# Down projection in a retention-plus-MLP kernel: a seven-product scheme exchanged for another with chained sums

## The chip, the cores and the metric

The kernel runs on one NeuronCore of one Trainium2 chip. TensorE (PE, with its weight loads listed apart as PEld) multiplies, VectorE (DVE) and ScalarE (ACT) do elementwise work and empty PSUM, GpSimd (POOL) issues the loads, and SyncE (SP) issues stores and DMA transposes. The metric is the device time in microseconds, the median of several executions. Before the change it is 288.92 us (288.50 to 289.43 over three executions).

## The reference

```python
# retention: batch 8, heads 8, seq 576, head dim 64
scores = q @ k.T / 8 * Dmat          # Dmat[i, j] = gamma_h ** (i - j) for i >= j, else 0
x = (scores @ v) -> [4608, 512]      # tokens x (heads * dim)
# MLP: d_model 512, d_ff 2048
h = x @ w_in                         # [4608, 2048]
g = h * sigmoid(1.702 * h)
out = g @ w_out                      # [4608, 512], float32
```

The change concerns only the last line, the down projection.

## The kernel before

The 4608 tokens are 36 units of 128, and four units make a chunk of 512 tokens, so there are nine chunks. The retention of later units is worked out ahead, in pieces placed between the products of the MLP (`block`, `ahead`). For a chunk the up projection (`up`, L560) takes 16 blocks f of 128 rows of d_ff: four matmuls for each f into PSUM bank A or B in turn, and then ACT's GELU (L569) from that bank into `gT[:, f, tokens]`. With two banks, block f+2 can only start when the GELU of block f has read its bank.

The down projection of chunk 0 is plain (`down`, L588). From chunk 1 on it works by seven products instead of eight. The g of a chunk is a 2x2 block matrix G: the row is the half of the tokens (`raw(row, ...)`), the column the parity of f. W (w_out) is a 2x2 block matrix too: the row is the parity of f, the column the half of the 512 outputs (`wpart`). A `product` (L673) is 16 matmuls of 128x256 for a pair of two units a half, eight matmuls for a pair of one unit a half; with `more` it is added onto what the bank holds. With `late=1` the matmuls that need the last f come at its end. `turn()` deals the banks A and B alternately. Chunks 1 to 7 are one `Pair` of two units in each half. Chunk 8 is two pairs with one unit in each half, and the last pair stores half rows (`halves=True`), those of row 1 through ACT's queue.

`run` (L701) is the order of the seven products. In the version before, the sums of w_out (`wsums`, five for each quarter of w_out, worked out during chunk 0) and of g (`sums`, five for each call: three into `gsum`, two in place in `gT`) are all independent of one another. In `run`, ACT copies three products or sums of products out of PSUM into `osb` (`copy`, L696), and DVE does six additions and subtractions (`comb`, L699), through a scratch tile `wtmp`. The last instruction on a pair's results is the `comb` of quarter (0, 0), on DVE.

Between the products stand the calls `hook(0)` to `hook(6)`. They issue pieces of the retention work: `x_out_pair` (L552), `scores_out` (L514) and `state_sum` (L449) on DVE, `state_cast` (L458) on ACT, and matmuls on PE. In chunks 2 to 7, `hook(0)` casts what was summed before, `hook(2)` issues a block on PE, hooks 2 to 5 two of its DVE pieces each, and `hook(6)`, behind the last product, calls `cast_now()`: a cast on ACT of the states of the next two units. That is one unit after chunk 2 (128x512) and two units after chunks 3 to 6 (128x1024); after chunks 1 and 7 hook 6 has no cast.

The order on each engine is the order in which the program calls `op`; there is no planner. `Program.op` (L41) derives the waits from the names that an operation reads and writes: every wait is a semaphore wait in front of the instruction. A value read from an earlier instruction of the same engine is waited for as well (except on PE); a mere overwrite on the same engine is not. An engine does not go past an instruction that waits. SP and ACT wait in the same way for the instruction that fills a row before they issue its store.

Of the kernel before, what the change touches and what calls it, by code (L numbers as in the profile page):

```python
# [17 lines left out]
NF = FF // P  # L18
# [11 lines left out]
class Program:  # L30
# [10 lines left out]
    def op(self, eng, fn, reads=(), writes=(), dma=None, ndma=1, after_ops=()):  # L41
        o = Op()
        o.eng, o.fn, o.dma, o.signal, o.count = eng, fn, dma, False, None
        o.idx = len(self.streams[eng]) + 1
        deps = {}
        for k in reads:
            for d in self.writers.get(k, ()):
                deps[id(d)] = (d, True)
        for k in writes:
            for d in self.writers.get(k, ()) + self.readers.get(k, ()):  # L50
                deps.setdefault(id(d), (d, False))
        known = self.known[eng]
        need = []
        for d, raw in deps.values():
            if d.dma is None:
                if d.eng == eng and dma is None and (eng == "pe" or not raw):
                    continue
                agent, val = d.eng, d.idx
            else:
                agent, val = d.dma, d.dval  # L60
            need.append((agent, val, d))
        for d in after_ops:
            need.append((d.eng, d.idx, d))
        need.sort(key=lambda x: -x[1])
        waits = {}
        for agent, val, d in need:
            if known.get(agent, 0) >= val:
                continue
            if agent in waits and waits[agent][0] >= val:
                continue  # L70
            waits[agent] = (val, d)
        pruned = []
        for agent, (val, d) in waits.items():
            if any(
                a2 != agent and d2.known.get(agent, 0) >= val
                for a2, (_, d2) in waits.items()
            ):
                continue
            pruned.append(d)
        for agent, (val, d) in waits.items():  # L80
            d.signal = True
            known[agent] = max(known.get(agent, 0), val)
            for a2, v2 in d.known.items():
                if v2 > known.get(a2, 0):
                    known[a2] = v2
        o.waits = pruned
        o.known = dict(known)
        if dma is None:
            o.known[eng] = max(o.known.get(eng, 0), o.idx)
        else:  # L90
            self.dma_count[dma] = self.dma_count.get(dma, 0) + 16 * ndma
            o.dval = self.dma_count[dma]
            o.known[dma] = o.dval
        self.streams[eng].append(o)
        for k in writes:
            self.writers[k] = (o,)
            self.readers[k] = ()
        for k in reads:
            self.readers[k] = self.readers.get(k, ()) + (o,)
        return o  # L100
# [60 lines left out]
def bass_retnet_parallel__then__act_gelu_quick_kernel(  # L161
# [10 lines left out]
    with es:  # L172
        def sb(name, shape, dtype):
            return es.enter_context(nc.sbuf_tensor(name, shape, dtype))
# [14 lines left out]
        xT = [sb(f"xT{i}", [P, 4, 512], BF16) for i in range(2)]  # L189
        gT = sb("gT", [P, NF, 512], BF16)  # L190
        gsum = sb("gsum", [P, 3, NF // 2, 256], BF16)
        wsum = sb("wsum", [P, 5, NF // 2, 256], BF16)
        wtmp = sb("wtmp", [P, 512], FP32)
        warmt = sb("warmt", [P, 512], BF16)
        tblt = sb("tblt", [P, 4], BF16)
        gq = sb("gq", [P, 6, 4, P], FP32)
# [16 lines left out]
        op = pr.op  # L213
# [381 lines left out]
        def store(u, n0=0, n1=DM, eng="sp"):  # L595
            i = u % 4

            def f(e):
                return [
                    e.dma_start(out[S * bb + s0 : S * bb + s0 + n, n0:n1], osb[p0 : p0 + n, i, n0:n1])  # L600
                    for p0, n, bb, s0 in unit_rows(u)
                ]
            o = op(eng, f, reads=okeys(i, n0, n1), writes=[f"out{u}_{n0}"],
                   dma=f"d_o{i}_{n0}", ndma=len(unit_rows(u)))
            last_store[o.dma] = o
# [13 lines left out]
        def wpart(r, c):  # L619
            return lambda k: (w_out_sb[:, 2 * k + r, 256 * c : 256 * c + 256], f"wout{k // 2}")  # L620

        def wsums(i):
            def part(r, c):
                return w_out_sb[:, 4 * i + r : 4 * i + 4 : 2, 256 * c : 256 * c + 256]

            for n, (x, y, alu) in enumerate((
                ((0, 0), (1, 1), ALU.add), ((0, 0), (0, 1), ALU.add), ((1, 0), (1, 1), ALU.add),
                ((0, 1), (1, 1), ALU.subtract), ((1, 0), (0, 0), ALU.subtract),
            )):
                op("dve", lambda e, n=n, x=x, y=y, alu=alu: e.tensor_tensor(  # L630
                    wsum[:, n, 2 * i : 2 * i + 2, :], part(*x), part(*y), alu),
                   reads=[f"wout{i}"], writes=[f"ws{n}_{i}"])

        def wsummed(n):
            return lambda k: (wsum[:, n, k, :], f"ws{n}_{k // 2}")

        class Pair:
# [14 lines left out]
                        for j in range(self.r[row], self.r[row] + self.nt)]  # L652

            def sums(self, f0, f1):
                a, g = (lambda r, c: self.gpart(r, c, f0, f1)), (lambda r, c: self.gkeys(r, c, f0, f1))
                for n, x, y in ((1, (1, 0), (1, 1)), (2, (0, 0), (0, 1)), (0, (0, 0), (1, 1))):
                    op("dve", lambda e, n=n, x=x, y=y: e.tensor_tensor(  # L657
                        gsum[:, n, f0 // 2 : f1 // 2, self.at : self.at + self.n], a(*x), a(*y), ALU.add),
                       reads=g(*x) + g(*y), writes=[f"gs{n}_{k}_{j}" for j in self.places() for k in range(f0 // 2, f1 // 2)])
                for x, y in (((1, 0), (0, 0)), ((0, 1), (1, 1))):  # L660
                    op("dve", lambda e, x=x, y=y: e.tensor_tensor(a(*x), a(*x), a(*y), ALU.subtract),  # L661
                       reads=g(*x) + g(*y), writes=g(*x))

            def raw(self, row, col):
                def f(k, t):
# [22 lines left out]
            def bank(self, b):  # L688
                return bank[b][:, 0 : 256 * self.nt].rearrange("p (t n) -> p t n", t=self.nt), [b]

            def tmp(self):
                w = wtmp[:, 2 * self.at : 2 * self.at + 256 * self.nt]
                return w.rearrange("p (t n) -> p t n", t=self.nt), [f"wtmp{j}" for j in self.places()]

            def copy(self, dst, src):
                op("act", lambda e: e.activation(dst[0], src[0], AF.Copy), reads=src[1], writes=dst[1])  # L696

# [3 lines left out]
            def run(self, c, hook, halves=False):  # L701

                a, b = turn(), turn()
                q, A, B, W = self.quarter, self.bank(a), self.bank(b), self.tmp()
                add, sub = ALU.add, ALU.subtract

                def give(row, col, whole):
                    for j in range(self.r[row], self.r[row] + self.nt):
                        if halves:
                            store(4 * c + j, 256 * col, 256 * col + 256, "act" if row else "sp")  # L710
                        elif whole:
                            store(4 * c + j)

                self.product(a, self.raw(1, 1), wsummed(4), late=1)
                self.copy(q(1, 1), A)
                hook(0)
                self.product(b, self.raw(0, 0), wsummed(3))
                self.comb(W, B, q(1, 1), add)
                hook(1)
                self.product(a, self.summed(1), wpart(0, 0), True)  # L720
                self.copy(q(1, 0), A)
                give(1, 0, False)
                hook(2)
                self.comb(q(1, 1), W, q(1, 0), sub)
                self.product(b, self.summed(2), wpart(1, 1), True)
                self.copy(q(0, 1), B)
                give(0, 1, False)
                hook(3)
                self.comb(q(0, 0), W, q(0, 1), sub)
                self.product(a, self.summed(0), wsummed(0))  # L730
                self.comb(q(1, 1), A, q(1, 1), add)
                hook(4)
                self.product(b, self.raw(1, 0), wsummed(1))
                self.comb(q(1, 1), B, q(1, 1), add)
                give(1, 1, True)
                hook(5)
                self.product(a, self.raw(0, 1), wsummed(2), True)
                self.comb(q(0, 0), A, q(0, 0), add)
                give(0, 0, True)
                hook(6)  # L740
                turn()

# [3 lines left out]
        def turn():  # L746
            turns[0] += 1
            return "BA"[turns[0] % 2]
# [351 lines left out]
```

## Time and profile before

| | |
|---|---|
| median of three executions | 288.92 us |
| the profiled execution, its own time | 290.05 us |
| its span, first to last instruction | 288.2 us |
| PE busy | 277.5 us, 96% |
| DVE busy | 187.8 us, 65% |
| ACT busy | 130.3 us, 45% |
| mean granted TensorE clock | 0.994 |
| sums of g (L657, L661) on DVE | 32.1 + 21.9 us |
| combinations (L699) on DVE, 54 of them | 34.0 us |
| copies (L696) on ACT, 27 of them | 14.8 us |

The 34.0 us are the five groups of L699 in the groups by line: 11.3 + 8.9 + 8.2 + 3.1 + 2.5. In such a listing a row has the line, the engine, what is written and read, the count, the time that the engine was busy with it, and the idle time ahead of it with what ended it. In a timeline a row has the start, the length, the engine, the line and the operation, and in brackets how long the engine had been idle and for whom. In the chain of waits a row has the start and the time that the step adds to the chain. The modelled end of a matmul lies past the start of the next one, so spacing on PE is read from starts.

### The profile page before, as it was taken

What the parts mean: (1) busy time and instruction counts of PE and PEld (TensorE: products, weight loads), DVE (VectorE), ACT (ScalarE), POOL (GpSimd) and SP (SyncE); (2) the same over time, 40 slices, a digit from 0 to 9 for tenths busy, and PEclk for the clock granted to TensorE, in tenths of its full rate; (3) what the DMA queues carried; (4) which work ended last, traced back from release to release, by engine and by line L of the source; (5) the groups of instructions that cost most, each with busy time, mean ns of one, the idle gap of its engine ahead of it and who ended that gap; (6) DMA issues with size and microseconds to landing.
All of it is one profiled execution on the core that took longest, in us unless ns stands there. A gap on an engine that the chain in (4) does not pass through costs nothing.

```text
span 288.2 us, 8995 instructions
## 1 busy us (share of the span) xinstructions
PE 277.5 (96%) x4018; PEld 179.4 (62%) x4018; DVE 187.8 (65%) x385; ACT 130.3 (45%) x230; POOL 110.3 (38%) x141
## 2 busy tenths in 40 slices
PE   8899999999869998999999999999999999999996
PEld 6575445888753487447944794478447834783385
DVE  6851757568858868477757785858486828553563
ACT  7556333663116541454165416541754075406721
POOL 9999888100880770049004910590053000000000
PEclk9999999999979999999999999999999999999999
DMA  9999999998999991779797997895879080003013
GB/s 169 175 207 206 200 236 248 236 145 194 101 230 236 113 189 27 209 105 190 84 238 83 147 123 218 106 199 67 238 87 119 2 218 2 2 12 136 0 39 109
DMA packets 116934, 40.69 MB, mean 141 GB/s; under 512 B 104096, under 2 KB 110240, under 8 KB 116896
## 3 DMA queue, kind: packets, MB, share of 16 engines
q0 software_dynamic: 79712, 22.82, 68.5%
q1 hardware_dynamic: 36896, 17.05, 23.0%
q8 instruction: 31, 0.51, 0.7%
q10 hardware_dynamic: 288, 0.26, 0.3%
q14 instruction: 7, 0.06, 0.1%
HBM read 36.70 MB, written 9.44 MB: 160 GB/s over the span
## 4 chain that ended last, share of the span: by engine, by line
PE 83%; POOL 7%; DMA 6%; DVE 2%; ACT 1%; issue 1%; POOLq 0%
PE psA L679 18%; PE psA L564 17%; PE psB L564 17%; PE psB L679 17%; DMA vn<-in_v_dram 6%; POOL w_in_sb L269 3%; PE psB L578 3%; PE psA L578 2%; POOL kqn L234 2%; PE psX L489 2%; POOL vn L247 1%; PE psB L590 1%; POOL w_out_sb L276 1%; PE psC L505 1%; PE psX L527 1%; PE psK L434 1%
## 5 line engine op out<-in xcount | busy, mean ns | idle before, releaser
L234 POOL DMA_DIRECT2D kqn<-in_k_dram x39 | 35.1, 908 | 107.6 <-DMA kqT<-kqn 105.3
L564 PE MATMUL psA<-xT,w_in_sb 128*128 128x512 bf16 x240 | 61.7, 380 | 0.0
L564 PE MATMUL psB<-xT,w_in_sb 128*128 128x512 bf16 x240 | 61.7, 379 | 0.0
L657 DVE TENSOR_TENSOR gsum<-gT 128x1024 bf16<-128x1024 bf16 (+1 forms) x66 | 32.1, 541 | 43.8 <-ACT gT L569 41.1
L569 ACT ACTIVATE gT<-psB 128x512 bf16<-128x512 f32 x60 | 35.8, 597 | 28.8 <-PE psB L564 28.5
L569 ACT ACTIVATE gT<-psA 128x512 bf16<-128x512 f32 x60 | 35.8, 597 | 22.5 <-PE psA L564 22.3
L564 PEld LDWEIGHTS psB<-xT,w_in_sb 128*128 128x128 bf16 x240 | 19.7, 97 | 31.2 <-ACT gT L569 14.2
L564 PEld LDWEIGHTS psA<-xT,w_in_sb 128*128 128x128 bf16 x240 | 19.4, 97 | 31.0 <-ACT gT L569 14.3
L247 POOL DMA_DIRECT2D vn<-in_v_dram x40 | 36.9, 937 | 0.2
L234 POOL DMA_DIRECT2D kqn<-in_q_dram x37 | 33.3, 912 | 0.3 <-issue 0.3
L679 PE MATMUL psA<-wsum,gT 128*128 128x256 bf16 x256 | 32.3, 280 | 0.0
L679 PE MATMUL psB<-wsum,gT 128*128 128x256 bf16 x256 | 31.0, 273 | 0.0
L458 ACT ACTIVATE kv<-stm 128x1024 bf16<-128x1024 f32 (+1 forms) x18 | 15.5, 863 | 29.8 <-DVE stm L449 29.8
L679 PEld LDWEIGHTS psA<-wsum,gT 128*128 128x128 bf16 x256 | 25.4, 101 | 4.6 <-ACT gT L569 1.0
L679 PEld LDWEIGHTS psB<-wsum,gT 128*128 128x128 bf16 x256 | 24.7, 98 | 4.3 <-ACT gT L569 1.5
L353 DVE TENSOR_TENSOR vp<-vn,vfac 128x512 bf16<-128x512 f32 x36 | 23.0, 683 | 4.6 <-DMA vn<-in_v_dram 4.6
L552 DVE TENSOR_TENSOR xT<-psX,gq 128x512 bf16<-128x512 f32 x16 | 11.0, 688 | 18.1 <-PE psX L527 18.0
L661 DVE TENSOR_TENSOR gT<-gT 128x1024 bf16<-128x1024 bf16 (+1 forms) x44 | 21.9, 538 | 0.0
L696 ACT ACTIVATE osb<-psA 128x512 f32<-128x512 f32 (+1 forms) x14 | 7.7, 551 | 28.0 <-PE psA L679 28.0
L679 PE MATMUL psA<-w_out_sb,gsum 128*128 128x256 bf16 x128 | 15.7, 273 | 1.0 <-issue 1.0
L696 ACT ACTIVATE osb<-psB 128x512 f32<-128x512 f32 (+1 forms) x13 | 7.1, 548 | 19.6 <-PE psB L679 19.6
L679 PE MATMUL psB<-w_out_sb,gsum 128*128 128x256 bf16 x128 | 15.5, 273 | 0.0
(107 smaller groups left out, 422.8 us busy)
## 6 DMA issues: line engine op xcount, KB each, us to landing
vn<-in_v_dram POOLq DMA_DIRECT2D x32, 256.0 KB, 5.3
out_dram<-osb SPq DMA_DIRECT2D x30, 256.0 KB, 2.3
kqn<-in_k_dram POOLq DMA_DIRECT2D x31, 128.0 KB, 5.1
kqn<-in_q_dram POOLq DMA_DIRECT2D x31, 128.0 KB, 5.1
w_out_sb<-in_moe_w_out_dram POOLq DMA_DIRECT2D x4, 512.0 KB, 13.7
out_dram<-osb SPq DMA_DIRECT2D x10, 128.0 KB, 2.3
w_in_sb<-in_moe_w_in_dram POOLq DMA_DIRECT2D x8, 128.0 KB, 5.0
w_in_sb<-in_moe_w_in_dram POOLq DMA_DIRECT2D x4, 256.0 KB, 7.7
```

The lines of the kernel that those rows point to most:

```text
L234: e.dma_start(kqn[sl][p0 : p0 + n, which, :, :], src[b, :, s0 : s0 + n, :].rearrange("h p d -> p h d"),)
L247: e.dma_start(vn[sl][p0 : p0 + n, :, :], v[b, :, s0 : s0 + n, :].rearrange("h p d -> p h d"))
L353: op(eng, lambda e: e.tensor_tensor(vp[u % NVP].ap(), vn[sl].ap(), vfac[:, ty, :, None].to_broadcast([P, H, DH]), ALU.mult), reads=[f"vn{s ...
L458: op("act", lambda e: e.activation(kv[:, i0 % NKV : i0 % NKV + n, :, :], stm[:, i0 % 8 : i0 % 8 + n, :, :], AF.Copy), reads=[f"stm{(i0 + i ...
L552: op("dve", lambda e: e.tensor_tensor(xT[ch % 2][:, slice(hh, 4, 2), P * jj : P * jj + 2 * P].rearrange("p g (u t) -> p u g t", u=2), ps32 ...
L564: op("pe", lambda e, a=a: e.matmul(bank[b][:, n0:n1], w_in_sb[:, a, P * f : P * f + P], xT[c % 2][:, a, n0:n1], start=(a == 0), stop=(a == ...
L569: op("act", lambda e: e.activation(gT[:, f, n0:n1], bank[b][:, n0:n1], AF.Gelu_apprx_sigmoid), reads=[b], writes=[f"g_{f}_{j}" for j in ra ...
L578: op("pe", lambda e, a=a, f=f, i=i: e.matmul(bank[b][:, n * i : n * i + n], w_in_sb[:, a, P * f : P * f + P], xT[c % 2][:, a, P * lo : P * ...
L657: op("dve", lambda e, n=n, x=x, y=y: e.tensor_tensor(gsum[:, n, f0 // 2 : f1 // 2, self.at : self.at + self.n], a(*x), a(*y), ALU.add), re ...
L661: op("dve", lambda e, x=x, y=y: e.tensor_tensor(a(*x), a(*x), a(*y), ALU.subtract), reads=g(*x) + g(*y), writes=g(*x))
L679: op("pe", lambda e, x=x, y=y, t=t, s=not more and t == 0 and k == 0, z=k == NF // 2 - 1: e.matmul(bank[b][:, 256 * t : 256 * t + 256], x, ...
L696: op("act", lambda e: e.activation(dst[0], src[0], AF.Copy), reads=src[1], writes=dst[1])
```

## The change

The seven products are formed in another way. The sums of w_out become four for each quarter, W01-W00, W11-(W01-W00), W11-W01 and W10-(W11-(W01-W00)); the second and the fourth read an earlier sum. The sums of g become four for each call, S1 = G10+G11, S2 = S1-G00, S3 = G00-G10 (in place) and S4 = G01-S2; S2 and S4 read an earlier sum. The first two products, G00 W00 and G01 W10, need no sums and both have `late=1`; together they are quarter (0, 0). Everything else accumulates on the two banks. ACT has four copies for a pair instead of three and DVE three combinations instead of six, and the scratch tile goes. The last operation on a pair's results is the copy of quarter (1, 0), on ACT, ahead of `hook(6)`. The row halves are stored in the opposite order: row 0 after the sixth product, row 1 after the seventh. The number and the shapes of the matmuls stay.

```diff
-        wsum = sb("wsum", [P, 5, NF // 2, 256], BF16)
-        wtmp = sb("wtmp", [P, 512], FP32)
+        wsum = sb("wsum", [P, 4, NF // 2, 256], BF16)
...
-            for n, (x, y, alu) in enumerate((
-                ((0, 0), (1, 1), ALU.add), ((0, 0), (0, 1), ALU.add), ((1, 0), (1, 1), ALU.add),
-                ((0, 1), (1, 1), ALU.subtract), ((1, 0), (0, 0), ALU.subtract),
-            )):
...
+            def ws(n):
+                return wsum[:, n, 2 * i : 2 * i + 2, :]
+
+            for n, x, y in ((0, part(0, 1), part(0, 0)), (1, part(1, 1), ws(0)),
+                            (2, part(1, 1), part(0, 1)), (3, part(1, 0), ws(1))):
+                op("dve", lambda e, n=n, x=x, y=y: e.tensor_tensor(ws(n), x, y, ALU.subtract),
+                   reads=[f"wout{i}"] + ([f"ws{n - 1}_{i}"] if n % 2 else []), writes=[f"ws{n}_{i}"])
...
-                for n, x, y in ((1, (1, 0), (1, 1)), (2, (0, 0), (0, 1)), (0, (0, 0), (1, 1))):
...
-                for x, y in (((1, 0), (0, 0)), ((0, 1), (1, 1))):
...
+                for d, kd, x, kx, y, ky, alu in (
+                    (s(0), ks(0), a(1, 0), g(1, 0), a(1, 1), g(1, 1), ALU.add),
+                    (s(1), ks(1), s(0), ks(0), a(0, 0), g(0, 0), ALU.subtract),
+                    (a(1, 0), g(1, 0), a(0, 0), g(0, 0), a(1, 0), g(1, 0), ALU.subtract),
+                    (s(2), ks(2), a(0, 1), g(0, 1), s(1), ks(1), ALU.subtract),
+                ):
...
-                self.product(a, self.raw(1, 1), wsummed(4), late=1)
-                self.copy(q(1, 1), A)
+                self.product(a, self.raw(0, 0), wpart(0, 0), late=1)
+                self.copy(q(0, 0), A)
                 hook(0)
-                self.product(b, self.raw(0, 0), wsummed(3))
-                self.comb(W, B, q(1, 1), add)
+                self.product(b, self.raw(0, 1), wpart(1, 0), late=1)
+                self.comb(q(0, 0), B, q(0, 0), ALU.add)
+                give(0, 0, False)
                 hook(1)
-                self.product(a, self.summed(1), wpart(0, 0), True)
+                self.product(a, self.summed(1), wsummed(1), True)
+                self.copy(q(0, 1), A)
+                hook(2)
+                self.product(b, self.summed(0), wsummed(0))
+                self.copy(q(1, 1), B)
+                hook(3)
+                self.product(a, self.raw(1, 0), wsummed(2), True)
+                self.comb(q(1, 1), A, q(1, 1), ALU.add)
+                give(1, 1, False)
+                hook(4)
+                self.product(b, self.summed(2), wpart(1, 1), True)
+                self.comb(q(0, 1), B, q(0, 1), ALU.add)
+                give(0, 1, True)
+                hook(5)
+                self.product(a, self.raw(1, 1), wsummed(3), True)
                 self.copy(q(1, 0), A)
-                give(1, 0, False)
-                hook(2)
-                self.comb(q(1, 1), W, q(1, 0), sub)
-                self.product(b, self.summed(2), wpart(1, 1), True)
-                self.copy(q(0, 1), B)
-                give(0, 1, False)
-                hook(3)
-                self.comb(q(0, 0), W, q(0, 1), sub)
-                self.product(a, self.summed(0), wsummed(0))
-                self.comb(q(1, 1), A, q(1, 1), add)
-                hook(4)
-                self.product(b, self.raw(1, 0), wsummed(1))
-                self.comb(q(1, 1), B, q(1, 1), add)
-                give(1, 1, True)
-                hook(5)
-                self.product(a, self.raw(0, 1), wsummed(2), True)
-                self.comb(q(0, 0), A, q(0, 0), add)
-                give(0, 0, True)
+                give(1, 0, True)
                 hook(6)
                 turn()
```

More of the change, by code (lines that the diff above doesn't have):

```diff
@@ L624, in part @@
                 return w_out_sb[:, 4 * i + r : 4 * i + 4 : 2, 256 * c : 256 * c + 256]
-            for n, (x, y, alu) in enumerate((
-                ((0, 0), (1, 1), ALU.add), ((0, 0), (0, 1), ALU.add), ((1, 0), (1, 1), ALU.add),
-                ((0, 1), (1, 1), ALU.subtract), ((1, 0), (0, 0), ALU.subtract),
-            )):
-                op("dve", lambda e, n=n, x=x, y=y, alu=alu: e.tensor_tensor(
-                    wsum[:, n, 2 * i : 2 * i + 2, :], part(*x), part(*y), alu),
-                   reads=[f"wout{i}"], writes=[f"ws{n}_{i}"])
+            def ws(n):
[4 more added lines that the diff above has]
+                   reads=[f"wout{i}"] + ([f"ws{n - 1}_{i}"] if n % 2 else []), writes=[f"ws{n}_{i}"])
         def wsummed(n):
@@ L654, in sums @@
             def sums(self, f0, f1):
+                k0, k1 = f0 // 2, f1 // 2
                 a, g = (lambda r, c: self.gpart(r, c, f0, f1)), (lambda r, c: self.gkeys(r, c, f0, f1))
-                for n, x, y in ((1, (1, 0), (1, 1)), (2, (0, 0), (0, 1)), (0, (0, 0), (1, 1))):
-                    op("dve", lambda e, n=n, x=x, y=y: e.tensor_tensor(
-                        gsum[:, n, f0 // 2 : f1 // 2, self.at : self.at + self.n], a(*x), a(*y), ALU.add),
-                       reads=g(*x) + g(*y), writes=[f"gs{n}_{k}_{j}" for j in self.places() for k in range(f0 // 2, f1 // 2)])
-                for x, y in (((1, 0), (0, 0)), ((0, 1), (1, 1))):
-                    op("dve", lambda e, x=x, y=y: e.tensor_tensor(a(*x), a(*x), a(*y), ALU.subtract),
-                       reads=g(*x) + g(*y), writes=g(*x))
+                s = lambda n: gsum[:, n, k0:k1, self.at : self.at + self.n]
+                ks = lambda n: [f"gs{n}_{k}_{j}" for j in self.places() for k in range(k0, k1)]
+                for d, kd, x, kx, y, ky, alu in (
[4 more added lines that the diff above has]
+                ):
+                    op("dve", lambda e, d=d, x=x, y=y, alu=alu: e.tensor_tensor(d, x, y, alu),
+                       reads=kx + ky, writes=kd)
             def raw(self, row, col):
@@ L689, in bank @@
                 return bank[b][:, 0 : 256 * self.nt].rearrange("p (t n) -> p t n", t=self.nt), [b]
-            def tmp(self):
-                w = wtmp[:, 2 * self.at : 2 * self.at + 256 * self.nt]
-                return w.rearrange("p (t n) -> p t n", t=self.nt), [f"wtmp{j}" for j in self.places()]
             def copy(self, dst, src):
@@ L703, in run @@
                 a, b = turn(), turn()
-                q, A, B, W = self.quarter, self.bank(a), self.bank(b), self.tmp()
-                add, sub = ALU.add, ALU.subtract
+                q, A, B = self.quarter, self.bank(a), self.bank(b)
                 def give(row, col, whole):
```

## The prediction

> **What bounds the kernel now.** I read the page first, then the longest waits, then the timelines of PE, ACT and DVE where chunk 3 ends and chunk 4 begins.
>
> ```profile
> PE 277.5 (96%) x4018; PEld 179.4 (62%) x4018; DVE 187.8 (65%) x385; ACT 130.3 (45%) x230; POOL 110.3 (38%) x141
> ...
> PEclk9999999999979999999999999999999999999999
> ...
> PE 83%; POOL 7%; DMA 6%; DVE 2%; ACT 1%; issue 1%; POOLq 0%
> ```
>
> PE is the bound, and its matmuls stay as they are in number and shape. What DVE is spared (one sum in five, half of the combinations) is worth nothing by itself; the time changes only where PE waits. Those waits are few:
>
> ```profile
> PE psX L489 <- ACT kv L458: 3.5, 2, 2.5
> ...
> PEld psA L564 <- DVE osb L699: 1.7, 4, 0.4
> ...
> PEld psB L564 <- DVE osb L699: 1.2, 3, 0.4
> ```
>
> The first row is chunk 1's retention blocks waiting for a cast, once 0.96 and once 2.51 us (behind the longer one the clock is at half, hence the 7 in PEclk). The other two are seven waits, one at the end of each of chunks 1 to 7: block f=1 of the next up projection waits for the last combination. Its place on three engines, between chunks 3 and 4, PE, then ACT, then DVE:
>
> ```profile
> 144.95 1.03 PE L564 MATMUL psB<-xT,w_in_sb 128*128 128x512 bf16 x4
> 145.90 1.04 PE L564 MATMUL psA<-xT,w_in_sb 128*128 128x512 bf16 x4
> 146.77 1.03 PE L564 MATMUL psB<-xT,w_in_sb 128*128 128x512 bf16 x4
> ...
> 144.91 1.06 ACT L458 ACTIVATE kv<-stm 128x1024 bf16<-128x1024 f32 x1 [4.41 <-DVE stm L449]
> 146.01 0.60 ACT L569 ACTIVATE gT<-psB 128x512 bf16<-128x512 f32 x1
> ...
> 143.40 0.69 DVE L699 TENSOR_TENSOR osb<-psB,osb 128x512 f32<-128x512 f32 x1 [0.24 <-PE psB L679]
> 144.01 0.41 DVE L449 TENSOR_TENSOR stm<-psK,stm 128x256 f32<-128x256 f32 x1
> 144.46 0.42 DVE L449 TENSOR_TENSOR stm<-psE,stm 128x256 f32<-128x256 f32 x1
> 145.15 0.69 DVE L699 TENSOR_TENSOR osb<-psA,osb 128x512 f32<-128x512 f32 x1 [0.27 <-PE psA L679]
> ```
>
> The reader should see two things. f=1 starts 0.95 after f=0, where the ordinary step is 0.865 (146.77 to 148.50 is two steps), so 0.09 is lost to the DVE combination that ends at 145.84, 0.06 before f=1 starts. And the cast of hook 6 runs on ACT during the seventh product, because ACT has nothing to do then; it is done just as the GELU of f=0 becomes ready.
>
> **The change, part by part.**
>
> *The last combination becomes a copy on ACT, in front of hook 6's cast.* This is the largest term. ACT takes its instructions in order, so the cast can no longer start at 144.91: it stands behind a copy that waits for the seventh product, until 145.15. These rows price the queue, the first two pairs for the spacings on ACT, the third for a cast that stands among the GELUs:
>
> ```profile
> 103.66 0.60 ACT L696 ACTIVATE osb<-psB 128x512 f32<-128x512 f32 x1 [1.15 <-PE psB L679]
> 104.16 1.05 ACT L458 ACTIVATE kv<-stm 128x1024 bf16<-128x1024 f32 x1
> ...
> 44.48 1.06 ACT L458 ACTIVATE kv<-stm 128x1024 bf16<-128x1024 f32 x1 [3.20 <-DVE stm L449]
> 45.44 0.58 ACT L611 ACTIVATE osb<-psA 128x512 f32<-128x512 f32 x1
> ...
> 90.53 0.62 ACT L458 ACTIVATE kv<-stm 128x512 bf16<-128x512 f32 x1
> ...
> 91.72 1.00 PE psB L564 x4
> ```
>
> Copy at 145.15; cast 0.50 later, 145.65; GELU of f=0 0.96 later, 146.61, to 147.21 instead of 146.61; f=2 needs its bank and starts 0.05 later, 147.26 instead of 146.77. That is +0.49. f=1 itself gains its 0.09 (the copy ends 0.60, not 0.69, after 145.15), but f=2 does not see it. f=3 waits for the GELU of f=1 (147.11 to 147.71), which is there before f=2 has run, so one stall a chunk. Hook 6 casts two units after chunks 3, 4, 5 and 6: 4 x 0.49 = +1.96. After chunk 2 it is one unit (0.63, spacing 0.52): copy 116.47, cast 116.97, GELU 117.49 to 118.09, f=2 at 118.14 instead of 118.09, +0.05. After chunks 1 and 7 there is no cast and the 0.09 is gained: -0.18. Together +1.83. Bounds for each of the four: 0.14, what the cast at 90.53 cost PE (a step of 1.00 instead of 0.86); and 0.70, if nothing overlapped on ACT (0.60 + 1.06 + 0.60 + 0.05 from 145.15 ends 0.69 late). I take 0.49, since its two spacings come from the same pairs of shapes.
>
> Here a rule speaks against the edit: the Trainium skill, "ScalarE: Activation LUTs", Rules for kernel authors, says to put additions and multiplications on VectorE, which it has up to three times faster in bf16. Here the rows have the copy from PSUM at 0.60 on ACT and the combination at 0.69 on DVE, so for a float32 source the row decides. If a copy were no shorter than a combination, all seven ends would lose 0.09 more and the sum below would be +2.1.
>
> *Sums of w_out, four for five, chained.* Only the last group has PE behind it:
>
> ```profile
> 39.47 1.75 DVE L630 TENSOR_TENSOR wsum<-w_out_sb 128x512 bf16<-128x512 bf16 x5
> 41.15 0.41 DVE L385 COPY kqT<-psE 128x512 bf16<-128x512 bf16 x1
> 41.48 0.68 DVE L353 TENSOR_TENSOR vp<-vn,vfac 128x512 bf16<-128x512 f32 x1
> ...
> PE psK L434 <- DVE vp L353: 0.2, 1, 0.2
> ```
>
> Five sums take 1.68 to the next start, 0.335 each. Chained work shows in the state sums: 144.01 to 144.46 is 0.45 for a 0.41 instruction, where unchained ones of that size follow each other after 0.335, so a wait for the neighbour costs 0.11. The second sum waits for the first; the fourth reads the second, with one between, as the combination at 141.69 did without a gap. Four sums take 1.45, the copy and the scaled v behind them come 0.23 earlier, and PE, which waited for both (0.09 and 0.15), gains 0.20. Bounds: 0 (the next load is late instead) and 0.23. A page differs: the Trainium skill, "VectorE: DVE Perf Modes", The DRAIN you can't avoid, has a semaphore between neighbours at no extra cost. The row says 0.11; by the page the group would end 0.34 earlier, the gain could be at most those 0.24, and the sum would be 0.04 lower.
>
> *Sums of g.* A call takes 0.61 + 0.72 + 0.61 + 0.61 = 2.5 instead of 3.1 us; S2 now waits for S1. Nobody waits: in chunk 3 the first sum starts at 132.31, so S2 is there at 133.7 (0.72 + 0.68 later), and the third product, which reads it, starts at 134.98. The first two products are the cover; they run from 131.48, and without them S2 would hold PE for 2.2 us. In the last chunk S1 starts at 273.94 and S2 ends at 274.55; the third product starts at 274.96. Price 0.
>
> *Combinations, six to three, and the bank waits.* The fourth, sixth and seventh products, and f=0, wait for a combination or a copy one product (1.75 us) older, as now. DVE's state sums in hooks 4 and 5 stay behind the combinations of the fifth and sixth products. So chunk 1's long wait stays: its cast (80.67) follows the state sum at 80.22, behind the combination at 79.16 of a product that ends at 79.12. The 0.96 wait stays too: that cast stands behind the copy of the fourth product, as before. In chunk 1 DVE does the scaling of v for units 12 and 13 some 2 us earlier; the loads for them were issued by 51, at a median of 12.9 us to landing, so it finds its data, and what is queued behind it on DVE (x_out at 75.59) waits for PE anyway. Price 0.
>
> *SP, POOL.* A row is stored after the sixth and one after the seventh product, as now; the row order changes, the count and the place on SP's queue do not, and so the transposes behind the stores and POOL's loads behind those stay. Price 0.
>
> *The end.* In the last chunk the first product takes 1.14 us, the following ones 1.04, since its last matmul needs the GELU of f=15 (ends 273.91). Now the first product reads even f only: -0.10. The last instruction is a copy of 0.38 instead of a combination of 0.42, and its store goes through ACT's queue, where the two of before landed in 1.7 to 1.8 us, as SP's last one: -0.04.
>
> **Sum**: +1.83 - 0.20 - 0.10 - 0.04 = +1.49. The profiled execution, 288.2 us of span and 290.05 in all, would become 291.54, its span 289.7. It is 1.13 longer than the median; on the median of 288.92 the same sum gives **290.4**. Its own range: +0.1 with four times 0.14 (289.0) to +2.5 with four times 0.70 and no gain in chunk 0 (291.5).
>
> **The rivals.**
> *Only the waits shrink* (the other side). If the GELU of f=0 were not late, all seven ends would gain 0.09 and the rest 0.34: 288.0. It decides if copy, cast and GELU end within 1.6 us of the seventh product's end (145.11); the rows make it 2.1. For it: ACT is 45% busy. Against: the order in its queue. 0.08.
> *Nothing reaches PE*: DVE was idle anyway and ACT's delay is taken up by slack that I overlook: 288.9. 0.08.
> *The half clock goes or comes*. It lasts 3.4 us after the 2.51 wait, and the seventh product takes 3.26 instead of 1.75; after the 0.96 wait the clock stayed full. If it goes: 290.4 - 1.5 = 288.9, 0.10. If a second one comes: 291.9, 0.06. The wait is the same, only 0.2 earlier.
> *S2 late*: a chained wait would have to cost over 1.4 us instead of 0.11; at 2 us eight downs would lose 0.6 each, 295. 0.03.
>
> **How the numbers follow.** The forecast has 0.65. The range 288.7 to 291.5 leaves out the gain (0.08), the second half clock and the late S2 (0.09). 0.3% of 288.92, 0.87 us, is about what this kernel's runs can tell from no change: faster is below 288.05, slower above 289.79. Faster 0.10 (the gain and 0.02 of the half clock). Same 0.20 (the 0.08, the other 0.08, 0.04 of the forecast's low end). Slower 0.70.
>
> **What would show it.** After chunks 3 to 6: copy, cast and GELU in a row on ACT, and a step of about 1.45 us on PE from f=1 to f=2; after chunks 1 and 7 a step of 0.865 from f=0 to f=1. DVE some 29 us less busy (a fifth of the 54.0 us of sums of g and of the 7.0 of w_out, half of the 34.0 of combinations), with none of it in the span. The scaled v near 41.3. It is wrong if the cast starts before the copy, or if the clock's row has no dip or two.

## The result and the profile after

The changed kernel takes 291.50 us at the median (289.55 to 294.63 over 12 executions), the kernel before 289.07 (288.50 to 289.90 over 12). The ratio is 1.0067, with a 95% interval of 1.0045 to 1.0088: slower by 1.9 us (1.3 to 2.5). The ratio leaves out the slowest execution, 294.63, which is more than 1.5% above the fastest; the medians alone are 2.4 us apart. The forecast was slower, at 290.4 with a range up to 291.5, so the measured median lies at the very edge of that range. From one execution to the next the changed kernel varies by more than the whole effect, so the cause has to be read inside the profile, stage by stage.

The profiled execution of the changed kernel took 289.83 us, its span is 288.0: 0.2 us *shorter* than that of the kernel before. Its page, in part:

```profile
PE 276.6 (96%) x4018; PEld 179.0 (62%) x4018; DVE 164.8 (57%) x332; ACT 133.5 (46%) x239; POOL 110.2 (38%) x141
...
PEclk9999999999999999999999999999999999999999
...
PE 76%; DMA 8%; POOL 7%; ACT 4%; DVE 2%; SPq 1%; issue 1%; POOLq 0%
```

DVE has 53 instructions and 23 us less to do, and PE is busy for as long as before. Two things are new in the page: the 7 in PEclk has gone, and ACT and DMA have a larger part of the chain that ended last. The list of the waits of PE says with what (sum in us, how many, the longest):

```profile
PE psC L504 <- DMA kqT<-kqn: 0.9, 2, 0.6
PE psB L563 <- ACT gT L568: 0.8, 2, 0.4
PE psA L563 <- ACT gT L568: 0.8, 2, 0.4
...
PEld psA L563 <- ACT osb L695: 1.3, 4, 0.3
```

The four waits for ACT's GELU, 0.4 us each, are new, and so is the wait for the transposed k and q (kqT). The same place as in the prediction, the end of chunk 3, on ACT, then on PE, now looks like this:

```profile
142.85 0.60 ACT L695 ACTIVATE osb<-psA 128x512 f32<-128x512 f32 x1 [4.64 <-PE psA L682]
143.34 1.05 ACT L457 ACTIVATE kv<-stm 128x1024 bf16<-128x1024 f32 x1
144.29 0.59 ACT L568 ACTIVATE gT<-psB 128x512 bf16<-128x512 f32 x1
144.77 0.60 ACT L568 ACTIVATE gT<-psA 128x512 bf16<-128x512 f32 x1
...
142.65 1.03 PE L563 MATMUL psB<-xT,w_in_sb 128*128 128x512 bf16 x4
143.51 1.03 PE L563 MATMUL psA<-xT,w_in_sb 128*128 128x512 bf16 x4
144.94 1.04 PE L563 MATMUL psB<-xT,w_in_sb 128*128 128x512 bf16 x4 [0.39 <-ACT gT L568]
```

Copy, cast and GELU stand in a row on ACT, with starts 0.49 and 0.95 apart. f=1 follows f=0 after 0.86 instead of 0.95; f=2 follows f=1 after 1.43 instead of 0.87.

What a stage costs is read best from the first matmul of one down projection to that of the next (us, from the starts on PE in the two traces):

| downs of chunks | 1 to 2 | 2 to 3 | 3 to 4 | 4 to 5 | 5 to 6 | 6 to 7 | 7 to 8 |
|---|---|---|---|---|---|---|---|
| before | 36.23 | 29.77 | 28.68 | 28.55 | 28.69 | 28.55 | 27.16 |
| after | 35.77 | 28.66 | 29.15 | 29.02 | 29.15 | 29.38 | 27.06 |

The columns with a cast of two units, 3 to 4 up to 6 to 7, grow by 0.47, 0.47, 0.46 and 0.83; of the last, 0.36 is a wait in chunk 6's block that the profile gives to no engine, and later runs do not have it there. The column without a cast, 7 to 8, falls by 0.10. So the ends cost 1.9 us, and the profiled pair hides that behind three other differences. In the first column the seventh product of chunk 1 ran at full clock and not at half, 1.4 us less, and chunk 2 then lost 1.1 us, most of it in the wait for kqT. In the second column the kernel before had a wait of 0.98 us that its profile calls "issue" and gives to no engine. And the first down of chunk 1 came 0.74 us earlier, only 0.08 of which lies in the sums of w_out, as shown further down.

### The profile page after: what moved, and what is told of

Same layout as the page of the kernel before. It is cut to its first block, busy times and chain, and to the rows that moved or that the text cites. A ratio compares the mean times of both kernels' runs of the same rounds, so it can differ in the third digit from the quotient of the medians.

```text
span 288.0 us, 8940 instructions
## 1 busy us (share of the span) xinstructions
PE 276.6 (96%) x4018; PEld 179.0 (62%) x4018; DVE 164.8 (57%) x332; ACT 133.5 (46%) x239; POOL 110.2 (38%) x141
## 4 chain that ended last, share of the span: by engine, by line
PE 76%; DMA 8%; POOL 7%; ACT 4%; DVE 2%; SPq 1%; issue 1%; POOLq 0%
PE psA L682 18%; PE psB L682 17%; PE psA L563 14%; PE psB L563 14%; DMA vn<-in_v_dram 6%; DMA kqT<-kqn 3%; POOL w_in_sb L268 3%; PE psB L577 3%; PE psA L577 2%; ACT kv L457 2%; POOL kqn L233 2%; PE psX L488 2%; ACT osb L695 1%; POOL vn L246 1%; PE psB L589 1%; POOL w_out_sb L275 1%
## 5 line engine op out<-in xcount | busy, mean ns | idle before, releaser
L664 DVE TENSOR_TENSOR gsum<-gT 128x1024 bf16<-128x1024 bf16 (+1 forms) x22 | 12.0, 544 | 53.4 <-ACT gT L568 50.2
L695 ACT ACTIVATE osb<-psA 128x512 f32<-128x512 f32 (+1 forms) x19 | 10.5, 552 | 44.0 <-PE psA L682 44.0
L695 ACT ACTIVATE osb<-psB 128x512 f32<-128x512 f32 (+1 forms) x17 | 9.3, 547 | 35.7 <-PE psB L682 35.7
L457 ACT ACTIVATE kv<-stm 128x1024 bf16<-128x1024 f32 (+1 forms) x18 | 15.5, 860 | 9.4 <-DVE stm L448 9.4
L682 PE MATMUL psA<-wsum,gT 128*128 128x256 bf16 x144 | 17.4, 273 | 0.0
L682 PE MATMUL psA<-wsum,gsum 128*128 128x256 bf16 x128 | 15.5, 273 | 0.0
L682 PE MATMUL psB<-wsum,gsum 128*128 128x256 bf16 x128 | 15.5, 273 | 0.0
L682 PE MATMUL psA<-w_out_sb,gT 128*128 128x256 bf16 x128 | 15.4, 273 | 0.0
L682 PE MATMUL psB<-w_out_sb,gT 128*128 128x256 bf16 x128 | 15.4, 273 | 0.0
L682 PEld LDWEIGHTS psA<-wsum,gT 128*128 128x128 bf16 x144 | 13.9, 98 | 1.7
L698 DVE TENSOR_TENSOR osb<-psB,osb 128x512 f32<-128x512 f32 (+1 forms) x14 | 8.9, 634 | 10.0 <-PE psB L682 10.0
```

Of the source, the lines that this page charges most:

```text
L457: op("act", lambda e: e.activation(kv[:, i0 % NKV : i0 % NKV + n, :, :], stm[:, i0 % 8 : i0 % 8 + n, :, :], AF.Copy), reads=[f"stm{(i0 + i ...
L664: op("dve", lambda e, d=d, x=x, y=y, alu=alu: e.tensor_tensor(d, x, y, alu), reads=kx + ky, writes=kd)
L682: op("pe", lambda e, x=x, y=y, t=t, s=not more and t == 0 and k == 0, z=k == NF // 2 - 1: e.matmul(bank[b][:, 256 * t : 256 * t + 256], x, ...
L698: op("dve", lambda e: e.tensor_tensor(dst[0], x[0], y[0], alu), reads=x[1] + y[1], writes=dst[1])
```

## The experiments

The theory was the prediction's: a copy on ACT in front of hook 6's cast makes the GELU of f=0 late. The rival came out of the profile above: the time comes from the DMA side, from loads and transposes that meet behind chunk 1, so that PE waits for kqT. Each ratio is to the kernel before, run on the same chip beside it.

**The cast in front of the copy.**

```diff
-                    if i == 6:
+                    if i == 6 or (i == 5 and c > 1):
                         cast_now()
```

> The changed kernel, but in chunks 2 to 7 the cast that stood at hook 6 is issued at hook 5, in front of the copy of quarter (1, 0) on ACT; nothing else differs. Theory 1 (the cast queued behind the copy is the cost): after chunks 3 to 6 the step on PE from block f=1 to f=2 falls from about 1.32 to 0.865 us, and the time falls by 1.8 to 1.9 us below the changed kernel's 291.5, to 289.6. Theory 2 (the time comes from the DMA side: loads and transposes that collide after chunk 1, with PE waiting for kqT): the steps shorten but the median stays within 0.5 us of 291.5.

Measured: ratio 1.0083 (1.0041 to 1.0126), median 291.33. Nothing was gained. Both theories had the steps shorten; the one from f=1 to f=2 did, to 0.87, but the one before it grew. ACT, then PE, at the end of chunk 3:

```profile
143.50 1.06 ACT L457 ACTIVATE kv<-stm 128x1024 bf16<-128x1024 f32 x1 [4.41 <-DVE stm L448]
144.46 0.58 ACT L695 ACTIVATE osb<-psA 128x512 f32<-128x512 f32 x1
144.94 0.59 ACT L568 ACTIVATE gT<-psB 128x512 bf16<-128x512 f32 x1
...
143.53 1.03 PE L563 MATMUL psB<-xT,w_in_sb 128*128 128x512 bf16 x4
145.09 1.04 PE L563 MATMUL psA<-xT,w_in_sb 128*128 128x512 bf16 x4 [0.54 <-ACT osb L695]
```

The cast cannot start before 143.50, when DVE's last state sum is done. Now the copy waits for the cast, and since f=1 needs the bank that the copy empties, f=1 is late, by 0.70 (a step of 1.56 instead of 0.86). The period from chunk 3's down to chunk 4's is 29.30 us, 0.15 longer than in the changed kernel. So the order on ACT is not the fault. Between the last state sum and the GELU of f=0 there is room for the cast and for nothing else; the fault is the copy being on ACT at all.

**The last copy on DVE.** This undoes one part of the change, the engine of the last operation:

```diff
-                self.copy(q(1, 0), A)
+                d, s = q(1, 0), A
+                if halves or self.nt == 1:
+                    self.copy(d, s)
+                else:
+                    op("dve", lambda e: e.tensor_copy(d[0], s[0]), reads=s[1], writes=d[1])
```

> The changed kernel, but the copy of quarter (1, 0) is done by DVE in chunks 1 to 7 (by ACT in chunk 8, as before); order and everything else unchanged. Theory 1, refined after the cast was put in front of the copy and f=1 became late instead of f=2 (ACT has more work there than fits, in whatever order): without the copy ACT starts the cast when the state sums end and the stretch from block f=0 to the next down is what it was before: 15.22 and 15.08 us in chunks 4 to 7 instead of 15.69 and 15.56, four times 0.47, so 1.8 us below the changed kernel, about equal to the kernel before (ratio 0.997 to 1.002). Theory 2 (the DMA side is the cost): the stretches shorten but the ratio stays at 1.006 or more.

Measured: ratio 0.9997 (0.9972 to 1.0022). The loss is gone. DVE's copy takes 0.69 us, and f=1 waits for it as it waited for the combination before. The periods of the four columns are 28.68, 28.55, 28.68 and 28.59, those of the kernel before. ACT has its old order of work, with the cast done when the GELU comes:

```profile
142.35 1.06 ACT L457 ACTIVATE kv<-stm 128x1024 bf16<-128x1024 f32 x1 [4.41 <-DVE stm L448]
143.45 0.60 ACT L568 ACTIVATE gT<-psB 128x512 bf16<-128x512 f32 x1
```

**One more ACT instruction in the kernel before.** This does the suspected part alone, with the old sums, products and combinations:

```diff
                 give(0, 0, True)
+                if not halves and self.nt == 2:
+                    src = q(0, 1)
+                    op("act", lambda e: e.activation(W[0], src[0], AF.Copy), reads=src[1], writes=W[1],
+                       after_ops=[pr.streams["pe"][-1]])
                 hook(6)
```

> The kernel before, with one more ACT instruction in chunks 1 to 7, of the size of a copy (128x512 float32 from osb to the scratch tile), in front of hook 6 and waiting for the last matmul of the seventh product; its result is not used. Theory 1: the ACT queue alone makes the loss, so the stretches of chunks 4 to 7 grow by 0.45 to 0.6 us each although sums, products, combinations are those of before: +1.9 to +2.4 us, ratio 1.0065 to 1.008. Theory 2: ratio 0.997 to 1.003.

Measured: ratio 1.0079 (1.0047 to 1.0111). The instruction costs the kernel before what the change costs it. ACT, then PE, at the end of chunk 3:

```profile
145.08 0.63 ACT L742 ACTIVATE wtmp<-osb 128x512 f32<-128x512 f32 x1 [4.64 <-PE psA L679]
145.62 1.04 ACT L458 ACTIVATE kv<-stm 128x1024 bf16<-128x1024 f32 x1
146.56 0.58 ACT L569 ACTIVATE gT<-psB 128x512 bf16<-128x512 f32 x1
...
145.83 1.04 PE L564 MATMUL psA<-xT,w_in_sb 128*128 128x512 bf16 x4
147.20 1.04 PE L564 MATMUL psB<-xT,w_in_sb 128*128 128x512 bf16 x4 [0.33 <-ACT gT L569]
```

The step from f=1 to f=2 is 1.37 us, the period 29.19. With the run before, the cause is shown from both sides: ACT's 0.6 us at this place are necessary for the loss and enough for it.

**The long wait of chunk 1, filled**, in both kernels (the eight matmuls work on zeros, and nothing reads their result):

```diff
                             state_cast(10, 12)
+                            warm(8, 'BA'[turns[0] % 2])
                             rest.extend(block(5, cast=False))
```

> The kernel before, with eight matmuls of 128x512 on zeros put into PE's long wait of chunk 1 (2.51 us before the block of hook 5), on the bank whose combination was just issued; results unused. Theory 1: the wait falls under 0.9 us, the half clock behind it goes and the seventh product takes 1.75 instead of 3.26, so chunk 2 begins 1.4 us earlier; the time falls by 1.4 to 1.5 us, to 287.6, if the half clock was there in most executions. Theory 2: the stores and the transposes behind them come 1.4 us earlier too and meet the loads, PE waits for kqT in chunk 2 instead, and the time is 288.6 to 289.5 with a larger spread.

> The changed kernel with the same eight matmuls in chunk 1's long wait. Theory 1: the executions that had the half clock lose it (1.4 us in those), and the difference to the kernel before with the same filling is the sum of the steps without the clock, +1.6 us or so. Theory 2: the spread of the changed kernel, 289.6 to 294.6, stays, because it comes from PE waiting for kqT behind loads, and the median stays at 291 to 292.

Measured: the kernel before with the filling 1.0005 (0.9974 to 1.0036), the changed kernel with it 1.0076 (1.0044 to 1.0109). In both profiles the wait at this place falls from 2.51 to 0.79 us, in front of the eight matmuls, and the seventh product of chunk 1 runs at full clock; chunk 1's down with its blocks takes 19.22 us, as in the profile after, instead of 20.80. The difference between the two kernels stays at 0.7%, so the clock has no part in it. The 1.4 us were nevertheless not gained by the kernel before, and theory 1 missed there. The dip is not in every execution: of the 23 executions of it that the ratio counts, 15 had a mean granted clock of 0.994 or less and 8 had 1.0. And the two groups are only 0.7 us apart at the median (289.39 and 288.68), so full clock in all of them would be worth some 0.5 us, which the interval (down to -0.75 us) does not exclude. Besides, the filling takes out only the dip in chunk 1: three of the 12 executions with it, the profiled one among them, still had a clock of 0.994 or less, and they were the slowest (291.0 to 291.3); in the profiled one the half clock stands in the lead-in, from 15.5 to 22.4 us. Neither profile waits for kqT in chunk 2, so theory 2's reason is not seen in them. Why the executions at full clock are only 0.7 us faster, and not 1.4, stays open.

**The loads of units 14 to 17 earlier.**

```diff
-                    load(u, after=[f"T{(4 * c + 9) % NQT}_0"])
+                    load(u, after=[f"T{(4 * c + (7 if c == 1 else 9)) % NQT}_0"])
```

> The changed kernel, but the loads of units 14 to 17 in chunk 1 wait for the transpose of unit 11 instead of 13. Theory 1: POOL starts them 2 to 3 us earlier, PE no longer waits for kqT in chunk 2 (0.9 us in the profile of the changed kernel), the stretch of chunk 2's up projection goes from 16.55 to 15.3 us; the median falls by 0.3 to 1 us, since the wait is there only in executions that reach chunk 2 early; the other 1.8 us stay. Theory 2 (DMA side is the cost): the median falls by 1.5 us or more and the spread of 3 to 5 us shrinks to that of before.

Measured: ratio 1.0033 (1.0000 to 1.0065), median 290.59. POOL starts the loads at 70.68 instead of 75.42 us, and PE no longer waits for kqT. The last loads that POOL issues and the four transposes that SP issues at the start of chunk 2 (start, time until the last is issued), first in the kernel before:

```profile
83.76 1.51 POOL L247 DMA_DIRECT2D vn<-in_v_dram  x2
88.11 5.36 SPq L399 DMA_TRANSPOSE kqT<-kqn  x4
```

Then in the changed kernel, and the transposes alone in this run:

```profile
85.94 1.52 POOL L246 DMA_DIRECT2D vn<-in_v_dram  x2
86.23 9.30 SPq L398 DMA_TRANSPOSE kqT<-kqn  x4
```

```profile
86.44 5.36 SPq L398 DMA_TRANSPOSE kqT<-kqn  x4
```

The period from chunk 1's down to chunk 2's falls from 35.77 to 34.57 us; the four columns of the ends stay as in the changed kernel (29.17, 29.03, 29.16, 29.08). So the ends cost the same without the wait for kqT, and the loss in chunk 2 appears where chunk 2 begins early or the loads late. The loads are released by the transpose of unit 13. That transpose landed 2.8 to 2.9 us after its issue in some profiles and 4.3 to 5.1 us in others, of old and new products alike, for no cause that the runs show, so its being late in the profile of the changed kernel is not the change's doing. Nor is the wait for kqT all that makes the changed kernel vary: with the loads earlier its executions still lie between 288.74 and 292.81 us.

**Both together, with chunk 1's sums earlier.** Three edits on the changed kernel: the loads as above, the last copy on DVE in chunks 2 to 6 (`if c in (1, 7, 8)` for ACT), and

```diff
                             rest.extend(block(4, cast=False))
+                            now(rest[:6])
+                            del rest[:6]
+                            state_cast(10, 12)
...
                             rest.clear()
-                            state_cast(10, 12)
                             rest.extend(block(5, cast=False))
```

> The changed kernel with three edits: the last copy on DVE in chunks 2 to 6, the loads of units 14 to 17 after the transpose of unit 11, and in chunk 1 the four state sums of units 10 and 11 and their cast issued at hook 3, ahead of the combination of the fifth product. By theory 1 the long wait of chunk 1 (2.51 us) falls to 0.5 or less, the half clock behind it goes (1.4 us), and the ends of chunks 3 to 6 cost nothing, so 3 to 4 us below the kernel before, ratio 0.986 to 0.990. If kqT sets a floor for chunk 2 that the earlier loads don't lower, chunk 2's up projection takes 17 to 19 us and the ratio is 0.995 to 1.0.

Measured: ratio 0.9864 (0.9833 to 0.9895), median 285.79: this version beats both kernels. The long wait is down to 0.4 (1.4 in all for the two blocks, the first still 0.96 or so), the clock has no dip in any execution, the executions lie within 1.6 us (285.02 to 286.55), and the period of chunk 1 to chunk 2 is 33.17.

**Without the earlier loads**, the same otherwise:

> The combined kernel without the earlier loads: the last copy on DVE in chunks 2 to 6, and in chunk 1 the four state sums and their cast at hook 3. If the arrival of kqT sets a floor for chunk 2 (PE cannot pass its block before the loads of units 14 to 17 have landed and been transposed), the 2 to 3 us gained in chunk 1 are waited for again in chunk 2: period from chunk 1's down to chunk 2's 34.5 to 37 us as in the changed kernel, instead of 33.2 in the combined one, and ratio 0.995 to 1.0. If there is no such floor: period 33.2 us, ratio 0.986 to 0.989.

Measured: ratio 1.0126 (1.0091 to 1.0160), the period 39.35 us. I had expected a floor: the gained time waited for again. It was worse than that. SP's transposes in chunk 2, in the timeline of this kernel and then of the combined one (start, time until the last is issued):

```profile
84.87 13.95 SPq L398 DMA_TRANSPOSE kqT<-kqn  x4
```

```profile
85.27 5.92 SPq L398 DMA_TRANSPOSE kqT<-kqn  x4
```

And PE's wait for them in this kernel, from the list of waits (sum in us, how many, the longest):

```profile
PE psC L504 <- DMA kqT<-kqn: 5.2, 2, 3.1
```

Issued while the loads are still running (POOL's loads start at 76.04 here and take 12 us to issue), the transposes take more than twice as long to go out. Against the changed kernel the first is issued 1.4 us earlier and the last lands 2.6 us later (101.35 and 98.78), with loads that start 0.6 us later. So arriving earlier, while the other queue was still loading, made the transposes later. The waits cost once more behind them: from 97.84 us the clock was at half for 3.41 us.

**Old products with the same edits around them.** The kernel before with the earlier loads and the earlier sums of chunk 1; then this kernel and the combined one again, side by side:

> The kernel before with two of the three edits of the combined kernel: loads of units 14 to 17 after the transpose of unit 11, and in chunk 1 the state sums of units 10 and 11 and their cast at hook 3. Theory 1: the gain of the combined kernel (ratio 0.986) comes from these edits and not from the new products; here two combinations more stand on DVE between the sums and the products, so the wait in chunk 1 is at most 0.6 us longer, the ends of chunks 1 to 7 each lose the 0.09 of before, and the ratio is 0.986 to 0.990. Rival (the new products, with DVE's load lower, are what let the edits work): ratio 0.995 to 1.0.

> The combined kernel once more, on the same chip as the next one, to compare new and old products with the same edits around them. Theory 1 (with the ACT queue out of the way, the new products save PE only the short waits: 0.20 in chunk 0, twice 0.09 at the ends of chunks 1 and 7, 0.10 in the last chunk): 0.3 to 0.6 us, 0.1 to 0.2%, less than the next one. Rival (the lighter DVE is worth more): 1 us or more less.

> The kernel before with the earlier loads and the earlier state sums of chunk 1, on the same chip as the one above. Theory 1: 0.3 to 0.6 us more than the combined kernel. Rival: 1 us or more above it.

Measured: 0.9909 (0.9882 to 0.9935) for the old products the first time; then, both on one chip: 285.84 us (285.48 to 286.36) for the new products and 286.37 (285.54 to 287.90) for the old, ratios 0.9896 (0.9869 to 0.9923) and 0.9920 (0.9892 to 0.9949). So most of the gain comes from the two edits in chunk 1 (the first time a little less of it than expected, 0.9909 where at most 0.990 was forecast). On one chip the new products then take off another 0.5 us, which is what the short waits promise (0.3 to 0.6). But the intervals overlap, and the runs on two chips (0.9864 and 0.9909) put 1.3 us between them, so the size is not settled, nor is the rival that the lighter DVE is worth more.

## Why the prediction was right

*The place and the mechanism.* The largest term was +1.83 us for the ends of the chunks. Its steps, against the profile after (starts on PE, us, f=0 to f=1 and f=1 to f=2):

| after chunk | before | forecast | measured |
|---|---|---|---|
| 1 and 7, no cast | 0.95, 0.87 | 0.86, 0.865 | 0.86, 0.86 |
| 2, cast of one unit | 0.95, 0.88 | 0.86, 1.0 | 0.86, 0.99 |
| 3 to 6, cast of two | 0.95, 0.87 | 0.86, 1.45 | 0.86, 1.42 |

The loss of each long end was 0.47, forecast 0.49. The runs changed one thing in its wording. I wrote that the cast is late *because* it stands behind the copy. Turned round, the copy is late because it stands behind the cast, and that costs 0.15 more. It is a matter of ACT's load in a window that the state sums open and the GELU closes.

*The rule of the Trainium skill* that was weighed there ("ScalarE: Activation LUTs", Rules for kernel authors: additions on VectorE) was set aside because a copy takes 0.60 on ACT and a combination 0.69 on DVE. The rows were right (a copy on DVE takes 0.69 too) and f=1 did gain its 0.09. Yet the copy on DVE, the slower engine for it, is 2.0 us better in the whole kernel (0.9997 against 1.0067). Here the engine that is free at the place counts, not the shorter instruction.

*The sums of w_out* were mis-sized, -0.20 forecast and about -0.08 measured. The last group and what follows it on DVE:

```profile
38.88 0.42 DVE L630 TENSOR_TENSOR wsum<-w_out_sb 128x512 bf16<-128x512 bf16 x1
39.33 0.42 DVE L630 TENSOR_TENSOR wsum<-w_out_sb,wsum 128x512 bf16<-128x512 bf16 x1
39.68 0.42 DVE L630 TENSOR_TENSOR wsum<-w_out_sb 128x512 bf16<-128x512 bf16 x1
40.13 0.42 DVE L630 TENSOR_TENSOR wsum<-w_out_sb,wsum 128x512 bf16<-128x512 bf16 x1
40.47 0.42 DVE L384 COPY kqT<-psE 128x512 bf16<-128x512 bf16 x1
```

The second sum starts 0.45 after the first, as forecast; but the fourth also starts 0.45 after the third, although the sum that it reads is one further back. So the step that failed is that a sum with one between would not wait. The group takes 1.59 us where I had 1.45, against 1.68 before. From the scaled v in front of the group to the next matmuls of the down on PE, in the chain that ended last, it is 3.92 us (37.94 to 41.86) instead of 4.00 (38.53 to 42.53).

*The sums of g* cost nothing, as forecast: S1 starts at 130.01, S2 0.73 later, and S2 is there at 131.43, before the third product that reads it (132.84 in the chain).

*The end*: the first product of the last chunk lost its 0.10. The tail did not lose 0.04; from the last matmul's end to the end of the span it is 2.69 us instead of 2.63.

*The rivals.* The half clock went in the profiled execution, as the third rival allowed. A clock row without a dip was also named as a sign that the prediction is wrong, and it is a large part (1.4 us) of why this execution took 289.83 and not the 291.54 forecast for it. That sign was badly chosen: the dip comes and goes in both kernels, and where chunk 1's was taken out of both the difference stayed. That the forecast for the median holds without a term for it rests on this, not on foresight. The S2 rival and the two in which nothing is lost fell. What no rival had was the wait for kqT in chunk 2. I had priced the queues of SP and POOL at nothing because the count and order of their work stay. The profile of the kernel before shows why that was thin: the issuing of its loads ended at 85.3 and its transposes began at 88.1, a gap of 2.8 us. In the profile after, the loads ended at 87.5 and the transposes began at 86.2. Of this shift of 4.1 us, 2.2 are loads that start later, behind the late transpose of unit 13, and 1.9 are transposes that start earlier, for the most part (1.4) because the half clock is missing.

*The sum.* Four times 0.47, +0.04, twice about -0.09, -0.10, -0.08 and +0.06 are +1.6, close to the +1.49 of the forecast; the measured 1.9 (1.3 to 2.5) holds both and leaves room for a few tenths of the wait in chunk 2, on which the forecast had put nothing. The earlier loads take about 1 us off the changed kernel (1.0067 to 1.0033), but the kernel before was not run with them alone, so how much of that 1 us is a loss that only the changed kernel has stays open. DVE's lighter work is worth nothing in the span, as forecast. It is 23 us less and not some 29: the combinations fell by 17 (34.0 to 17.1), as forecast, the sums by only about 6 instead of 12.

## What to carry to other kernels

Where one engine is full and the others have time on average, look at the seams: between two stages an idle-looking engine may have a window exactly as long as the work already in it, and an instruction moved there is paid for in full by the engine that is the bound. Before moving an operation for its shorter duration, list what the receiving engine does in that very microsecond, and what it must have finished for whom. And before gaining time in one stage, look at what the transfers of the next one run into when they start earlier.

## What the runs showed of the hardware that was not expected

- Transposes by DMA and loads issued by POOL slow each other, and by how much goes with their distance. In the 13 profiles the four transposes of chunk 2 go out in 5.4 to 5.9 us when the last load was issued 2.3 us or more before them, in 6.7 to 7.5 us at 0.6 to 1.4 us, and in 8.1 to 14 us when loads are still being issued. The last load lands 5.0 us after its issue in the profile before, 8.2 in the profile after and 10.9 in the slowest case. PE waited up to 5.2 us in all for the transposes.
- The wait of 2.51 us in chunk 1 was followed by 3.4 us at half clock in the profile before and by none in the profile after. The Trainium skill, "TensorE: Matmul & The Clock Gate", Part 1, gives a free-running activity window of 3.4 us, and the clock records of these profiles agree with it: where they show a change of the clock, the stretches between changes are whole multiples of 3.41 us (78.51, 3.41 and then full clock in the profile before; 92.16 and 3.41 without the earlier loads). Laid on this grid, in the six profiles that have the wait at its full 2.51 us, it falls wholly into one window in the two profiles that have the dip (79.28 to 81.78 in a window from 79.21 to 82.63 before; likewise with one more ACT instruction), and is cut in two by a window's edge in the four that don't, with at most 1.71 us in one window (1.65 and 0.86 in the profile after). So whether this wait costs clock depends on where it falls on the grid, which differs from one execution to the next.
- A wait on DVE for a sum two instructions back cost as much (0.11 us) as one for the sum just before, in all four groups of w_out's sums, whose instructions are 0.42 us long. In the sums of g it cost nothing, with instructions of 0.69 us (131.35 to 131.95 in the profile after, the usual 0.60) or of 0.29 us (263.95 to 264.16, the usual 0.21). Why, the runs do not show.
